# Linear attention and a two-layer MLP on one core: a decode without its magnitude pass, a later range check, and a rewoven first stage

## The chip, the core and the metric

The kernel runs on one NeuronCore of one Trainium2 chip. The metric is device microseconds of one execution. In the profile PE is TensorE's matmul row and PEld its weight loads; DVE is VectorE, ACT ScalarE, POOL GpSimd, and SP the engine that issues most DMAs. Each engine executes its own list of instructions in order.

## The reference

```python
batch, n_heads, seq, head_dim = (4, 8, 768, 48)          # q, k, v, f_logit in float32
f = 1.0 / (1.0 + np.exp(-f_logit))
for t in range(S):
    state = f[:, :, t, :, None] * state + einsum('bhd,bhe->bhde', k[:, :, t], v[:, :, t])
    y[:, :, t] = einsum('bhd,bhde->bhe', q[:, :, t], state)
x = y.transpose(0, 2, 1, 3).reshape(3072, 384)
h = x @ w_in                                              # w_in 384 x 2048
return (maximum(h, 0) ** 2 @ w_out).astype(float32)       # w_out 2048 x 384
```

`w_in` and `w_out` arrive as float64, so the kernel receives them as 64-bit words and has to turn them into float32 itself.

## The kernel before

**Tiling.** The sequence of 768 positions is cut into 6 blocks of 128 (times 4 batches: 512 columns). A unit is one block and one pair of heads (hp): unit n is block n // 4, pair n % 4; units 0 to 3 are block 0, units 4 to 7 block 1. A unit's attention is worked in two chunks of 64 positions: scores inside a chunk, a carried state between chunks. The MLP keeps all weights in SBUF, split into a high and a low part (fp32r), and forms each product of two split numbers from three matmuls. The hidden layer has 16 slices f of 128; a slice's first layer ("up") is 9 matmuls of 128x512, its second layer ("down") 9 more. For block 0, slices 0 and 1 take 3 further matmuls with a fourth weight piece (w4), since block 0's fourth pair of heads is not yet spread over the other x tiles then.

**Decoding a weight** (`decode`, `bits`, `halves`). One 128x384 weight piece comes as 64-bit words, 384 KB. Pieces are numbered (f, i), i = 0 for the first layer and 1 for the second. An early piece costs: on ScalarE a pass |upper word| * 2^-112 with a running sum for a later range check (L138), and a pass that builds the top bits from one byte (L140); on VectorE two shift-and-or passes (L143, L149); on ScalarE a copy to the high part (L166); on VectorE a subtraction for the low part (L168). Late pieces, decoded inside the flow, take L138 and three VectorE passes.

**An order written out by hand.** TensorE, VectorE, ScalarE and SP execute in the order of the program text. Until the MLP is under way, that order is two strings of tokens, FIRST and SECOND; `step` turns each token into instructions. The number is the unit, the slice or the piece:

- `busy`n: n transposes of the identity into an unused bank of TensorE
- `f k L v`: loads of gate logits, keys and queries, all three, values; `j i o`: loads of w4, first-layer and second-layer pieces
- `G` gates (ScalarE); `K` a scan and a product for the keys (VectorE), with a maximum on POOL (L454); `Q` reciprocal, scan and product for the queries (VectorE; the reciprocal needs POOL's maximum)
- `T` transposes of the keys, `N` their copies (ScalarE), `D` state additions, `S` scores, `Y` outputs (TensorE); `M` mask, `C` states (VectorE)
- `r s` crossings: copies of queries and states to the other half of the partitions (ScalarE for block 0, SP DMAs for block 1); `m` moves the fourth pair's share (DMA)
- `H` high part of x (ScalarE), `z` subtracts it by a matmul with a negative identity, `X` low part (ScalarE after a `z`, else VectorE); `h g` spread the fourth pair over the x tiles (DMA)
- `e n t a w`: decode w4; `A I V c J` and `B O Z d P`: the five steps of decoding a first-layer and a second-layer piece, in the order above (J and P are the subtractions)
- `u U` up, `R` square (three ScalarE passes), `E` rest (VectorE subtraction of the high part, L258), `W` down, for block 0's slices 0 to 5

**The flow** (`flow`). After SECOND the three sums of block 0 are copied aside (`keep`, L322), and 90 steps follow: block 1's 16 slices, block 0's other 10, then blocks 2 to 5. Step n does up, square and rest of its slice, and down of the slice two steps back. Two PSUM banks hold the up sums, so up of step n + 2 needs the rest of step n. Everything else hangs on hooks at (step, place): place 0 ahead of up, 0.5 after the squares, 0.7 after rest, 1 after down. Late pieces are decoded there, and the attention of blocks 2 to 5 sits in slots (SLOTS: steps 12, 15, 18, ..., 35, 39, 43, 47, 51, 55, ...), with its loads six steps ahead, gates and keys three ahead, queries and transposes one ahead. In the slot the old unit's outputs and the new one's scores share TensorE; then come the old unit's H and X (and `h g`, the DMAs x<-ys, when the old unit is a block's fourth pair: steps 23, 39, 55), the new one's r, M, C and m.

At the end of the last pass one flag tells whether the inputs were in range; if not, a general path runs (it doesn't here).

Of the kernel before, what the change touches and what calls it, by code (L numbers as in the profile page):

```python
# [22 lines left out]
P = 128  # L23
# [18 lines left out]

LAG = 2
# [19 lines left out]
j0 e0 n0 f0 busy11 busy3 G0 busy2 k0 t0 K0 T0 f1 k1 Q0 G1 v0 K1 S0 N0 D0 M0 i0 A0 I0 T1 L2 o2 L4 C0  # L63
Q1 r0 s0 G2 K2 v1 Y0 N1 H0 z0 X0 D1 S1 B2 i3 Q2 T2 busy3 m1 C1 a0 S2 A3 w0 v2 o1 N2 r1 D2 G4 I3 i1
M1 s1 K4 v3 A1 Y1 D3 H1 C2 s2 z1 X1 r2 m0 f5 m2 S3 r3 o0 B0 V0 M2 k5 L6 v5 busy3 Y2 H2 Q4 r4 v4 C3 s3
G5 I1 T4 z2 X2 M3 busy9 Y3 c0 N4 K5 G6 Q5 V1 H3 busy5 z3 X3 T5 S4 D4 o3 i5 o5 i2 B3 J0 m4 r5 B1 C4 c1 s4 u0
O0 U0 M4 Y4
"""
SECOND = """
J1 Z0 u1 V3 R0 K6 H4 X4 N5 D5 S5 E0 T6 d0 P0 A2 C5 c3 U1 O1 I2 W0 R1 N6 J3 M5 h3 Z1 d1 s5  # L70
Y5 Q6 H5 X5 V2 c2 E1 g3 U3 P1 A5 v6 o4 S6 D6 M6 i4 J2 r6 C6 m5 I5 R3 E3 A4 W1 V5 O3 I4 c5 J5 U2 R2
m6 O2 V4 Z2 s6 v7 r7 Y6 H6 c4 X6 E2 J4 U5 d2 D7 S7 P2 U4 M7 C7 Z3 B4 B5 R4 s7 W2 O4 O5 d3 Z4 Z5 d4
d5 P3 Y7 E4 H7 X7 g7 h7 P4 R5 E5 W3 W4 P5 W5
# [3 lines left out]
class Moe:  # L77


    def __init__(self, ctx, tc, const, sums, out):  # L80
        self.tc, self.nc, self.sums, self.out = tc, tc.nc, sums, out

        self.const, self.raw, self.w, self.ps, self.turns = const, {}, {}, {}, 0
        self.xs, self.spares, self.w4, self.homes, self.held = [], 0, None, {}, None

        self.floor = const.tile([P, 1], F32, name="floor")
        tc.nc.vector.memset(self.floor, -31.0 / 64.0)
# [26 lines left out]
    def decode(self, f, i, scr, early):  # L114

        if early:
# [3 lines left out]
        total = self.sums[:, 2 * f + i : 2 * f + i + 1]  # L120
        yield from self.bits(self.raw[f, i], a, total, early)
        yield from self.parts(f, i, a)

    def bits(self, st, a, total, early):
# [12 lines left out]
        kw = {} if total is None else {"accum_out": total}  # L137
        nc.scalar.activation(a, upper_f, AF.Abs, scale=2.0**-112, **kw)  # L138
        if early:
            nc.scalar.activation(lower, first, AF.Identity, scale=2.0**-5, bias=self.floor[: st.shape[0]])  # L140
        yield
        if early:
            nc.vector.scalar_tensor_tensor(  # L143
                out=h, in0=h, scalar=3, in1=lower, op0=ALU.logical_shift_left, op1=ALU.bitwise_or
            )
        else:
            nc.vector.tensor_scalar(out=h, in0=h, scalar1=3, scalar2=None, op0=ALU.logical_shift_left)
# [4 lines left out]
        if not early:  # L152
            nc.vector.scalar_tensor_tensor(  # L153
                out=h, in0=lower, scalar=29, in1=h, op0=ALU.logical_shift_right, op1=ALU.bitwise_or
            )
# [8 lines left out]
    def halves(self, w, a):  # L164
        nc = self.nc
        nc.scalar.copy(out=w[:, 0], in_=a)  # L166
# [94 lines left out]

    def down(self, f, es=range(NJ)):
# [17 lines left out]
    def flow(self, passes, hooks, opened, closed, held=False):  # L280
# [7 lines left out]
        if held:  # L288
            passes[-1].ends = passes[-1].fs[-2:]
            downs.update({size - 2: [], size - 1: [size - 4, size - 3], size + 1: []})  # L290
        for n in range(size + LAG):
            if n < size:
                self.cur, f = row[n]
                if f == self.cur.fs[0]:
                    opened(self.cur)
                for hook in hooks.get((n, 0), ()):
                    hook()
                self.up(f)
                self.square(f, self.held if held and n == size - 1 else None)
                for hook in hooks.get((n, 0.5), ()):  # L300
                    hook()
                self.rest(f)
                for hook in hooks.get((n, 0.7), ()):
                    hook()
            for m in downs.get(n, ()):
                self.cur, f = row[m]
                if f == self.cur.fs[0]:
                    self.sums_of()
                self.down(f)
                if f == self.cur.fs[-1]:  # L310
                    closed(self.cur)
            for hook in hooks.get((n, 1), ()):
                hook()

    def keep(self):

        part = [
            self.gp.tile([P, NT], F32, tag=f"part{e}", name=f"part{self.cur.blk}_{e}", bufs=1)
            for e in range(NJ)
        ]  # L320
        for e in range(NJ):
            (self.nc.vector.tensor_copy if e % 2 else self.nc.scalar.copy)(out=part[e], in_=self.cur.po[e])  # L322
        return part
# [40 lines left out]
def fast_path(ctx, psum, tc, moe, ident, low, flag, fkqT, vN, w, w4, out):  # L364
# [32 lines left out]
    G.memset(last_kn, 0.0)  # L397

# [7 lines left out]
    class Unit:  # L406
# [74 lines left out]
        def across(self, out, in_, by_dma):  # L481


            (nc.sync.dma_start if by_dma else nc.scalar.copy)(out=out, in_=in_)

        def crossed(self):
            self.rx = self.wk([ROWS, B * C], "rx", 2)
            for c in range(self.blk == 0, NC):
# [4 lines left out]
                    self.blk == 1,  # L493
                )

        def crossed_states(self):
            for c in range(self.blk == 0, NC):
                r = (1 - c) * C
                self.across(self.sx[c * C : c * C + D], self.sp[r : r + D, c], self.blk == 1 and self.hp > 0)
# [132 lines left out]

        def less(self):


            for c in range(NC):
                nc.tensor.matmul(
                    self.py[:, c], lhsT=minus, rhs=self.y[0][:, c], start=False, stop=True,
# [3 lines left out]
        def lower(self):  # L642
            hi, lo = self.y
            if self.blk == 0:
# [13 lines left out]
        def stage(self, letters):  # L658
# [99 lines left out]
    def step(t):  # L758
# [8 lines left out]
        nm = t.rstrip("0123456789")  # L767
        n = int(t[len(nm) :])
        if nm == "busy":
            if 0 not in moe.cur.ph:  # L770
# [338 lines left out]
```

## Time and profile before

| | us |
|---|---|
| median of 3 runs (lowest to highest) | 490.5 (490.15 to 491.19) |
| the profiled execution, its own time | 489.16 |
| its span, first to last instruction | 487.5 |
| PE busy, of the span | 472.8 |
| DVE / ACT / POOL busy | 256.5 / 281.7 / 32.1 |

PE's busy time is modelled: matmuls are pipelined, a 128x512 matmul lasts about 0.39 us in the rows, while its successor begins earlier. In the profile's 40 slices of the span PE stands at 9 tenths or more from the fourth slice on; DVE falls from 9 to 1 tenth over the span.

### The profile page before, as it was taken

The page shows a single profiled execution, that of the slowest core. Times are in us where ns is not written, and L with a number is a line of the kernel's source. Part 1 is how long each engine was busy: PE and PEld are TensorE (multiplying, and loading weights), DVE is VectorE, ACT ScalarE, POOL GpSimd, SP SyncE. Part 2 cuts the span into 40 slices and gives each one's busy share as a digit, 9 for nine tenths or more (in the row PEclk, how much of TensorE's full clock was granted, in tenths as well). Part 3 has the DMA queues.
Part 4 walks back from the last instruction along what each step waited for, and adds up shares of the span by engine and source line. Part 5 has one row for each costly group of instructions (what it writes and reads, how often), then busy time and mean ns, then how long its engine had stood idle before and what let it go on. Part 6 is the DMA issues. An engine that isn't in the chain of part 4 may idle for free. (4 is left out here: it accounts for less than half of the span.)

```text
span 487.5 us, 11465 instructions
## 1 busy us (share of the span) xinstructions
PE 472.8 (97%) x4795; PEld 388.2 (80%) x4795; DVE 256.5 (53%) x474; ACT 281.7 (58%) x570; POOL 32.1 (7%) x82
## 2 busy tenths in 40 slices
PE   5889999999999999999999999999999999999996
PEld 5677787888788888888888888888888888888884
DVE  7999966989985355643437443346343212221111
ACT  4777757887676555644546645555655444544451
POOL 6222010001100000000000000000000000000000
PEclk9999999999999999999999999999999999999998
DMA  8985235566134004232005222004210002100002
GB/s 284 309 284 143 58 103 197 205 200 224 29 95 143 17 6 119 94 101 74 1 2 125 94 93 82 1 1 117 87 26 2 2 0 34 66 0 3 0 0 71
DMA packets 22636, 42.60 MB, mean 87 GB/s; under 512 B 4512, under 2 KB 8128, under 8 KB 22576
## 3 DMA queue, kind: packets, MB, share of 16 engines
q1 hardware_dynamic: 22128, 40.86, 27.1%
q0 software_dynamic: 448, 0.92, 0.8%
q8 instruction: 39, 0.64, 0.5%
q14 instruction: 21, 0.17, 0.1%
HBM read 31.69 MB, written 4.72 MB: 75 GB/s over the span
## 5 line engine op out<-in xcount | busy, mean ns | idle before, releaser
L241 PE MATMUL ph<-x,w 128*128 128x512 f32 x864 | 216.4, 395 | 1.8 <-DVE gl L258 1.4
L241 PEld LDWEIGHTS ph<-x,w 128*128 128x128 f32 x864 | 159.4, 188 | 36.5 <-DVE w L168 1.1
L268 PE MATMUL po<-gh,w 128*128 128x512 f32 x570 | 175.6, 389 | 0.0
L258 DVE TENSOR_TENSOR gl<-ph,gh 128x512 fp32r<-128x512 f32 x95 | 65.6, 691 | 172.1 <-ACT gh L253 171.8
L251 ACT ACTIVATE ph<-ph 128x512 f32<-128x512 f32 x96 | 55.9, 582 | 119.7 <-PE ph L241 119.5
L268 PEld LDWEIGHTS po<-gh,w 128*128 128x128 f32 x570 | 107.0, 188 | 22.2
L268 PE MATMUL po<-gl,w 128*128 128x512 f32 x285 | 111.1, 390 | 0.0
L268 PEld LDWEIGHTS po<-gl,w 128*128 128x128 f32 x285 | 53.5, 188 | 11.2
L252 ACT ACTIVATE ph<-ph 128x512 f32<-128x512 f32 x96 | 55.9, 582 | 3.0
L253 ACT CAST gh<-ph 128x512 fp32r<-128x512 f32 x95 | 55.8, 587 | 3.0
L449 DVE TENSOR_TENSOR_SCAN fkq<-fz,dr 128x520 f32<-128x520 f32 x18 | 22.3, 1236 | 6.3 <-ACT fz L444 6.3
L166 ACT CAST w<-wa 128x384 fp32r<-128x384 f32 (+1 forms) x33 | 16.6, 511 | 15.3 <-DVE wa L153 12.3
L454 POOL TENSOR_SCALAR fkq<-fkq 128x8 f32<-128x8 f32 x18 | 13.2, 735 | 145.1 <-DVE fkq L449 136.6
L463 DVE TENSOR_TENSOR_SCAN fkq<-fz,dz 128x520 f32<-128x520 f32 x18 | 22.3, 1242 | 0.6
L602 PE MATMUL ab_False<-sc,vn 64*48 64x64 f32 (+1 forms) x480 | 20.7, 220 | 0.0
L138 ACT ACTIVATE wa<-raw 128x384 f32<-128x384 f32 (+1 forms) x33 | 18.1, 548 | 4.3 <-DMA raw<-in_w_dram 4.2
L631 ACT CAST x<-ab_False 112x512 fp32r<-112x512 f32 x12 | 7.0, 587 | 22.0 <-PE shared L537 16.0
L611 PE MATMUL ab_False<-rx,sx 48*48 48x64 f32 (+1 forms) x240 | 19.4, 216 | 0.0
L647 DVE TENSOR_TENSOR x<-ab_False,x 112x512 fp32r<-112x512 f32 x12 | 8.3, 692 | 20.2 <-ACT x L631 20.2
L149 DVE SCALAR_TENSOR_TENSOR wa<-raw,wa 128x384 int32<-128x384 int32 (+1 forms) x33 | 17.9, 551 | 0.7
L602 PEld LDWEIGHTS ab_False<-sc,vn 64*48 64x48 f32 (+1 forms) x480 | 18.0, 126 | 0.0
L168 DVE TENSOR_TENSOR w<-wa,w 128x384 fp32r<-128x384 f32 (+1 forms) x33 | 17.9, 545 | 0.0
(138 smaller groups left out, 461.5 us busy)
## 6 DMA issues: line engine op xcount, KB each, us to landing
raw<-in_w_dram SPq DMA_DIRECT2D x32, 384.0 KB, 4.3
fkq<-in_fkqT_dram SPq DMA_DIRECT2D x15, 768.0 KB, 5.8
vn<-in_vN_dram SPq DMA_DIRECT2D x24, 192.0 KB, 4.5
out_dram<-ob SPq DMA_DIRECT2D x14, 256.0 KB, 2.4
fkq<-in_fkqT_dram SPq DMA_DIRECT2D x9, 256.0 KB, 4.6
x<-ys SPq DMA_DIRECT2D x30, 64.0 KB, 2.4
last_kq<-fkq SPq DMA_DIRECT2D x28, 64.5 KB, 2.3
out_dram<-part SPq DMA_DIRECT2D x3, 256.0 KB, 2.4
```

The costliest lines, as they stand in the source:

```text
L138: nc.scalar.activation(a, upper_f, AF.Abs, scale=2.0**-112, **kw)
L149: nc.vector.scalar_tensor_tensor(out=h, in0=upper, scalar=-(1 << 31), in1=h, op0=ALU.bitwise_and, op1=ALU.bitwise_or)
L241: self.nc.tensor.matmul(self.cur.ph[f], lhsT=w[:, i], rhs=x[:, j], start=first and n == 0, stop=last and n == 2)
L251: nc.scalar.activation(ph, ph, AF.Relu)
L252: nc.scalar.activation(ph, ph, AF.Square)
L253: nc.scalar.copy(out=gh, in_=ph)
L258: self.nc.vector.tensor_tensor(out=gl, in0=self.cur.ph.pop(f), in1=gh.bitcast(F32), op=ALU.subtract)
L268: self.nc.tensor.matmul(c.po[e], lhsT=l, rhs=r, start=f == c.fs[0] and i == 0, stop=f in c.ends and i == 2, skip_group_check=len(c.ends) > 1,)
L449: V.tensor_tensor_scan(out=rr[:, ::-1], data0=self.fz[:, NZ * CZ : 0 : -1], data1=dr[:, ::-1], initial=0.0, op0=ALU.mult, op1=ALU.add,)
L463: V.tensor_tensor_scan(out=pp, data0=self.fz[:, : NZ * CZ], data1=dz, initial=0.0, op0=ALU.mult, op1=ALU.add)
L602: nc.tensor.matmul(to[:m], lhsT=self.vn[rows, b, h * D : h * D + m], rhs=self.sc[rows, h, b], start=b == 0, stop=none and c == 0 and b == ...
L611: nc.tensor.matmul(to[:m], lhsT=s[rows, b * D : b * D + m], rhs=q[rows], start=False, stop=b == B - 1,)
```

## The change

1. **Early pieces without the magnitude pass.** `bits` for an early piece no longer issues L138; its ScalarE pass writes the top bits straight into the output, and two VectorE passes combine them with the upper word.
2. **A later check.** The 12 early pieces are remembered; in the flow, at steps 32, 34, ..., 54, the words of one piece are loaded again (two DMAs of 256 KB and 128 KB), and at steps 34, 36, ..., 56, place 0.7, VectorE masks the exponents and takes a minimum and a maximum. `verdict` compares these with two bounds.
3. **More matmuls with the negative identity.** Units 4 and 5 get a `z` too, so their `X` goes to ScalarE; slices 0, 1 and 3 of block 0 use `F` (one matmul) and `l` (a ScalarE copy) in place of `E`.
4. **Crossings of block 1** go to ScalarE; a mark ' at a token sends three of the high-part copies (d3', d4', d5') to VectorE, and lets B5' use another scratch buffer.
5. **The order.** FIRST and SECOND are new; `flow` yields between its parts, so that tokens `x` run its first parts inside SECOND, and `p` makes the copies of `keep` one by one. The loads of slices 6 and 7 are tokens now.

```diff
 FIRST (after):
+f0 busy11 G0 j0 k0 v0 f1 busy3 v1 e0 k1 K0 L2 n0 L4 o0 busy4 G1 Q0 busy4 T0 busy4 N0 D0
+K1 S0 C0 Q1 T1 i0 N1 D1 G2 M0 s0 r0 S1 K2 G4 Y0 busy4 v2 t0 H0 r1 busy4 B0 T2
+A0 Q2 N2 z0 D2 M1 v3 C1 busy4 X0 S2 C2 f5 I0 i1 s1 v5 Y1 i3 busy4 m2 G5 O0 busy3
+r2 V0 H1 m0 z1 A1 M2 D3 i2 X1 o1 v4 s2 k5 m1 K4 r3 c0 Y2 C3 S3 a0 i5 L6
+H2 M3
 SECOND (after):
+z2 T4 J0 I1 s3 X2 Y3 A3 H3 A2 N4 w0 z3 V1 X3 o2 u0 Q4 K5 U0 D4 c1 r4 J1
+C4 S4 M4 R0 B1 v6 Z0 u1 s4 Y4 h3 d0 I2 T5 H4 N5 Q5 F0 z4 X4 o3 l0 I3 P0
+r5 V3 o5 U1 G6 i6 D5 C5 S5 s5 i4 M5 R1 c3 W0 Y5 K6 J3 V2 F1 H5 l1 c2 T6
+Q6 N6 J2 v7 O1 m6 o4 g3 z5 U3 X5 m5 i7 D6 S6 C6 A5 U2 r6 M6 R3 o6 Z1 F3
+I5 s6 Y6 d1 P1 A4 H6 W1 m4 V5 I4 B2 X6 c5 V4 D7 l3 J5 R2 C7 S7 r7 U5 s7
+M7 E2 c4 O2 J4 Y7 Z2 B3 H7 U4 d2 O3 X7 B5' P2 h7 W2 B4 Z3 O4 d3' P3 O5 R4
+R5 Z4 d4' E4 P4 E5 Z5 W3 W4 g7 o7 d5' P5 x1 x2 x3 x4 W5 p1 p2 p0 x6 x7 x8
+x9 x10 x12 x13 x14 x15 x16 x17 x18 x19 x20 x21 x22 x23
@@ bits @@
-        nc.scalar.activation(a, upper_f, AF.Abs, scale=2.0**-112, **kw)
         if early:
-            nc.scalar.activation(lower, first, AF.Identity, scale=2.0**-5, bias=...)
+            nc.scalar.activation(h, first, AF.Identity, scale=2.0**-5, bias=...)
+            yield
+            nc.vector.scalar_tensor_tensor(
+                out=h, in0=upper, scalar=3, in1=h, op0=ALU.logical_shift_left, op1=ALU.bitwise_or)
+            yield
+            nc.vector.scalar_tensor_tensor(
+                out=h, in0=upper, scalar=(1 << 30) - 1, in1=h, op0=ALU.bitwise_or, op1=ALU.bitwise_and)
+            yield
+            return
@@ halves @@
-        nc.scalar.copy(out=w[:, 0], in_=a)
+        (nc.vector.tensor_copy if self.second else nc.scalar.copy)(out=w[:, 0], in_=a)
+        self.second = False
@@ new in Moe @@
+    def less(self, f, minus):
+        gh, _ = self.cur.g[f]
+        self.nc.tensor.matmul(self.cur.ph[f], lhsT=minus, rhs=gh, start=False, stop=True, ...)
+    def rest_less(self, f):
+        _, gl = self.cur.g[f]
+        self.nc.scalar.copy(out=gl, in_=self.cur.ph.pop(f))
+    def check_load(self, w):
+        f, i = self.unchecked.pop(0)
+        self.words2 = []
+        for n, cut in enumerate((slice(0, 256), slice(256, DM))):
+            t = self.gp.tile([P, NT], F32, tag=f"part{n}", name=f"check{n}_{f}_{i}", bufs=1)
+            t = t[:, : 2 * (cut.stop - cut.start)]
+            self.nc.sync.dma_start(t.bitcast(I64), w[f, i][:, cut])
+            self.words2.append((t, cut))
+    def check(self):
+        nc, n = self.nc, self.checked
+        self.checked += 1
+        a = self.gp.tile([P, NT], F32, tag="part2", name=f"checked{n}", bufs=1)[:, :DM]
+        words, self.words2 = self.words2, ()
+        for t, cut in words:
+            upper = t.bitcast(I32).rearrange("p (n two) -> p n two", two=2)[:, :, 1]
+            nc.vector.tensor_scalar(out=a.bitcast(I32)[:, cut], in0=upper, scalar1=EXPONENTS, ...)
+        for k, op in enumerate((ALU.min, ALU.max)):
+            at = 2 * LO * k + n
+            nc.vector.tensor_reduce(out=self.ends[:, at : at + 1], in_=a, axis=..., op=op)
@@ fast_path @@
+    G.memset(moe.sums, 0.0)
+    G.memset(moe.ends, 1.0)
+        for k in range(2 * LO):
+            n = CHECKS + 2 * k                       # CHECKS = 32
+            hook(n, 0.5, lambda: moe.unchecked and moe.check_load(w))
+            hook(n + 2, 0.7, lambda: moe.words2 and moe.check())
```

## Rows read from the trace of the kernel before

**Rows 1.** Busy time by stretch; columns PE, PEld, DVE, ACT, POOL, clock, DMA.
```profile
4.40:34.10 29.70, 23.73 (x565) 19.19 (x563) 27.91 (x45) 20.03 (x48) 9.03 (x18) 1.00 0.95 309
34.10:74.10 40.00, 39.11 (x582) 30.87 (x577) 33.65 (x71) 27.85 (x62) 5.40 (x11) 1.00 0.43 122
160.00:480.00 320.00, 320.00 (x2966) 264.62 (x2964) 122.07 (x203) 165.90 (x309) 9.89 (x31) 1.00 0.15 43
```

**Rows 2.** Timeline of PE; columns start, length, line, instruction, count, idle before.
```profile
1.59 3.67 PE L773 MATMUL ph<-ident 128*128 128x128 f32 x16 [1.59 <-POOL ident masks.py:199]
...
9.60 1.13 PE L553 MATMUL ds<-fkq 48*64 48x64 f32 x32 [1.23 <-DVE fkq L466]
...
20.81 0.69 PE L553 MATMUL ds<-fkq 48*64 48x64 f32 x32
...
30.06 0.34 PE L602 MATMUL first_py<-sc,vn 64*48 64x64 f32 x9 [0.39 <-DVE sc L567]
...
31.89 0.49 PE L637 MATMUL first_py<-ys,minus 112*112 112x256 f32 x2
32.23 0.60 PE L511 MATMUL pk<-ident,fkq 128*128 128x128 f32 x4
...
34.14 0.50 PE L241 MATMUL ph<-x,w 128*128 128x512 f32 x1
35.12 2.14 PE L241 MATMUL ph<-x,w 128*128 128x512 f32 x8 [0.47 <-DVE w L168]
...
71.95 4.24 PE L241 MATMUL ph<-x,w 128*128 128x512 f32 x18
76.79 2.37 PE L241 MATMUL ph<-x,w 128*128 128x512 f32 x9 [0.59 <-DVE gl L258]
```

**Rows 3.** Timeline of DVE in the first stage.
```profile
22.14 1.24 DVE L449 TENSOR_TENSOR_SCAN fkq<-fz,dr 128x520 f32<-128x520 f32 x1 [0.32 <-ACT fz L444]
...
24.03 0.35 DVE L582 TENSOR_TENSOR sp<-ds,fkq 112x192 f32<-112x192 f32 x1
...
24.68 0.55 DVE L149 SCALAR_TENSOR_TENSOR wa<-raw,wa 128x384 int32<-128x384 int32 x1
25.16 0.68 DVE L567 TENSOR_TENSOR sc<-ds,mask 128x512 f32<-128x512 f32 x1
25.75 0.20 DVE L461 RECIPROCAL dz<-fkq 128x8 f32<-128x8 f32 x1
...
27.87 0.35 DVE L582 TENSOR_TENSOR sp<-ds,last_kq 112x192 f32<-112x192 f32 x1
...
34.52 0.55 DVE L168 TENSOR_TENSOR w<-wa,w 128x384 fp32r<-128x384 f32 x1
...
68.83 0.55 DVE L168 TENSOR_TENSOR w<-wa,w 128x384 fp32r<-128x384 f32 x1
```

**Rows 4.** Timeline of POOL at the first maximum.
```profile
6.63 0.67 POOL L454 TENSOR_SCALAR fkq<-fkq 128x8 f32<-128x8 f32 x1 [0.33 <-POOL x L697]
```

**Rows 5.** Instructions of line L147 on DVE; ns minimum, median, maximum.
```profile
L147 DVE TENSOR_SCALAR wa<-wa x20: 350/353/360, 76.6 to 134.7; 128x384 int32<-128x384 int32 x20
```

**Rows 6.** Groups by line on ACT, 0 to 74.1 us; busy, mean ns, idle before.
```profile
L138 ACT ACTIVATE wa<-raw 128x384 f32<-128x384 f32 (+1 forms) x13 | 7.1, 550 | 4.3 <-DMA raw<-in_w_dram 4.2
```

**Rows 7.** Timeline of SP's queue near step 39 of the flow.
```profile
256.58 3.75 SPq L654 DMA_DIRECT2D x<-ys  x6
...
261.65 0.60 SPq L437 DMA_DIRECT2D fkq<-in_fkqT_dram  x1
```

**Rows 8.** DMA issues by line: count, KB each, median us to landing.
```profile
out_dram<-ob SPq DMA_DIRECT2D x14, 256.0 KB, 2.4
...
fkq<-in_fkqT_dram SPq DMA_DIRECT2D x9, 256.0 KB, 4.6
```

**Rows 9.** Timeline of DVE at step 40 of the flow.
```profile
260.78 1.24 DVE L449 TENSOR_TENSOR_SCAN fkq<-fz,dr 128x520 f32<-128x520 f32 x1 [0.75 <-ACT fz L444]
```

**Rows 10.** Timeline of PE behind step 42 of the flow.
```profile
267.50 0.60 PE L511 MATMUL shared<-ident,fkq 128*128 128x128 f32 x4
```

More of the change, by code (lines that the diff above doesn't have):

```diff
@@ L151, in bits @@
         )
[L152 to L155, printed above, removed]
+        nc.vector.scalar_tensor_tensor(
+            out=h, in0=lower, scalar=29, in1=h, op0=ALU.logical_shift_right, op1=ALU.bitwise_or
+        )
         yield
@@ L305, in flow @@
             for m in downs.get(n, ()):
-                self.cur, f = row[m]
-                if f == self.cur.fs[0]:
+                c, f = row[m]
+                self.cur = c
+                if f == c.fs[0]:
                     self.sums_of()
                 self.down(f)
[L310 to L323, printed above, removed]
+                if f == c.fs[-1]:
+                    closed(c)
@@ new lines, in flow, with keep @@
+            at(n, 1)
+            yield
+    def keep(self, part, e):
+        ob = self.gp.tile([P, NT], F32, tag=f"part{e}", name=f"part{self.cur.blk}_{e}", bufs=1)
+        (self.nc.vector.tensor_copy if e % 2 else self.nc.scalar.copy)(out=ob, in_=self.cur.po[e])
+        part[e] = ob
+    def check_load(self, w):
[6 more added lines that the diff above has]
+            self.words2.append((t, cut))
@@ L325, in finish @@
+    checked, words2 = 0, ()
     def finish(self, dst, part=None, third=None):
@@ L773, in step @@
                 nc.tensor.transpose(out=moe.cur.ph[0][:, 0:P], in_=ident, identity=ident)
+        elif nm == "x":
+            next(row)
+        elif nm == "p":
+            moe.cur = first
+            moe.keep(part, n)
         elif nm in ("i", "o"):
@@ L784, in step, with product @@
             if nm in "AB":
-                decoding[n, i] = moe.decode(n, i, pro, True)
+                decoding[n, i] = moe.decode(n, i, pro, True, not mark)
+            if nm in "cd":
+                moe.second = bool(mark)
             next(decoding[n, i])
-        elif nm == "u":
+        elif nm in "uURFlEW":
+            moe.cur = first
+            product(nm, n)
+        else:
+            unit(n).stage(nm, mark)
+    def product(nm, n):
+        if nm == "u":
             moe.up(n, last=False)
@@ L814, in fast_path @@
         moe.sums_of()
-        for t in SECOND.split():
-            step(t)
-        part = moe.keep()
         whole = half[0] + half[1]
@@ L894, in fast_path @@
         moe.hold()
-        moe.flow(passes, hooks, opened, closed, held=True)
+        row = moe.flow(passes, hooks, opened, closed, held=True)
+        for t in SECOND.split():
+            step(t)
+        for _ in row:
+            pass
         return passes[-1], read[0]
@@ L1016, in block @@
             c = moe.begin(nm, x, list(range(NF)), sums)
-            moe.flow([c], {}, lambda c: None, closed, held)
+            for _ in moe.flow([c], {}, lambda c: None, closed, held):
+                pass
         with tc.For_i(0, NBLK - 1, 1) as blk:
```

113 lines of the change are left out of this document (68 added, 45 removed).

## The prediction

> **What bounds the kernel now.** I read the busy times by stretch first. From 160 us to 480 us TensorE is busy for 320.00 of 320 us, while VectorE works 122 us and ScalarE 166 us of them [rows 1]. Nothing that shortens another engine's list there can show, and an addition to one shows only if it makes TensorE wait. The stretch from 4.4 to 34.1 us is the opposite: VectorE is busy for 27.91 of 29.70 us, and TensorE's 23.73 us hold padding. From 34.1 to 74.1 us both are close to full, 39.11 and 33.65 of 40 us [rows 1].
>
> The list of TensorE's instructions gives the places [rows 2]. It begins with 16 padding transposes. The first product of block 0's first layer starts at 34.14 us and its run stalls 0.47 us on a weight, so the dense work starts in effect at 34.61 us. Block 1's flow starts at 71.95 us; its third group waits 0.59 us. The time is therefore the moment at which dense work starts, plus TensorE's work, plus stalls. VectorE's list sets that moment.
>
> **Prices on VectorE** come from one unbroken stretch, start to start [rows 3]: K (scan and product) 24.03 - 22.14 = 1.89 us; C in block 0 0.65; one shift-and-or of a weight 0.48; M (mask) 0.59; Q (reciprocal, scan, product) 27.87 - 25.75 = 2.12. The three passes of the 112x256 weight I take at 256/384 of 0.48, 0.32 each.
>
> **Start of the dense work.** Before, VectorE's list up to the step J0 that the stall waits for has 5 K (9.45), 5 Q (10.60), 4 M (2.36), 4 C (2.60), three small passes (0.96), 5 shift-ors (2.40) and J0 (0.48): 28.85 us, done at 34.52 + 0.55 = 35.07 [rows 3]. So 6.2 us are start and gaps. The new order asks less before u0: u0 stands behind z3, which follows Y3, which needs M3. Up to M3 VectorE has 4 K (7.56), 3 Q (6.36), 4 M (2.36), 4 C (2.60), two small passes (0.64) and 3 shift-ors (1.44): 20.96 us. I keep 6.2 us of start and gaps. The load f0 now goes ahead of the weight load j0, but Q0 needs POOL's maximum, which began at 6.63 us right behind POOL's own clearing of x and took 0.67 us [rows 4]. Two more clearings now stand ahead of it, so the early load buys between 0.2 us lost and 0.8 us gained; I take nothing. M3 ends at 27.2. Before, Y3 started at 30.06 and z3 started at 31.89 with 0.34 us until the next transposes at 32.23 [rows 2]: 2.2 us, and about 0.2 us between M3 and Y3. The new u0 starts at 27.2 + 0.2 + 2.2 = 29.6 us, 5.0 us earlier.
>
> **What that moves behind it.** T5, D4 and S4 ran before u0 and now run after: 34.14 - 32.23 = 1.9 us, a wait of about 0.2 in it, so 1.7 us. New on TensorE are three products F (18 products take 4.24 us from 71.95 us on, so (4.24 - 0.39)/17 = 0.226 us each) and z4, z5 (0.34 each): 1.4 us. Together +3.1 us.
>
> **Stalls.** TensorE idles 40.00 - 39.11 = 0.89 us in the second stretch [rows 1], 0.47 of it already counted; the other 0.42 and the 0.59 us at 76.79 us can go, since x2 now puts block 1's first group ahead of W5, and x3 its squares ahead of the copies p. That is -1.0 us. New stalls come from the two lists running side by side. TensorE's list from 29.6 us: 71.95 - 34.61 - 0.42 = 36.9 before, plus 3.1, plus 2.0 for block 1's first group, ends at 71.6 us. VectorE's after M3: 69.4 (68.83 + 0.55, the early stage's last weight part) - 35.07 [rows 3] = 34.3 us before; plus Q4, K5, Q5, two shift-ors, one small pass and J0 (7.9); minus five passes of about 0.6 us that go to ScalarE (E0, E1, E3, X4, X5; 3.0); plus three copies d3', d4', d5' at 0.35 to 0.55 us, taken as 0.4, near the one-source pass of the same 128x384 [rows 5]: 1.2. That makes 40.4 with its old waits inside, so P5 at 67.6 us, when W5 needs it by 69.6. Two lists with 2 us to spare in 40 will hold each other up: between 0 and 3 us; I take 0.5, since the old pair lost 0.4. The early stage in sum: -5.0 + 3.1 - 1.0 + 0.5 = -2.4 us.
>
> **Edits that I cost at nothing.** The magnitude pass is 13 x 0.55 = 7.1 us of ScalarE [rows 6], which has 20.0 of 29.7 and 27.9 of 40 us filled before 74.1 us [rows 1]; it hides behind VectorE and TensorE. The room is used: 14 crossings of block 1 go from SP's queue to ScalarE, each smaller than that pass, so under 7.7 us, and five of VectorE's passes join them. If ScalarE were late instead, one of its waits, at most 0.55 us each, would show at the bank of a product. Fourteen fewer DMAs on SP free its queue; the weight loads i6 to o7, which only the flow decodes, move up into that room.
>
> **The later check.** Eleven checks run at steps 34 to 54 of the flow, some 230 to 320 us into the span (an estimate, from 72 us at step 0 and 258 at step 40): twelve loads are made, but the load at step n stands ahead of the check of the same step and replaces the words list, so each check reads the words loaded in its own step. One check is one AND over 384 columns in two pieces and two reductions. The trace has no such reduction; between the one-source pass (0.35 us [rows 5]) and a shift-or (0.48) for each of the three it is 1.1 to 1.5 us, 12 to 16 us in all. VectorE has 198 free us in 160 to 480 us; without that cover all of it would show.
>
> The order of SP's queue is another matter. At step 39 SP issues six x<-ys at 256.58 us behind VectorE's ys, then two moves, and its next load went out at 261.65 us [rows 7]. The check's two loads of step 40 stand exactly there: 261.65 and 262.25. A 256 KB transfer lands 2.4 us (writes) to 4.6 us (fkq) after its issue [rows 8]: 264.7 to 266.9 for the second. VectorE, which executes in order, stands at that check from about 260 us on. Queued behind it are K of the next unit, at 260.78 us before [rows 9], and the rest pass of step 41. After landing there remain 0.9 to 1.3 us of check and 1.89 of K, so K ends at 267.5 to 270.1; TensorE's transposes of that K ran at 267.50 and the product whose bank the rest pass frees right behind them [rows 10]. The price is 0.2 (0.7 for the rest pass, 0.5 of it covered) to 2.9 us; I take 1.2, a landing near 3.3 us. No other of the checked steps has six x<-ys ahead of its loads; step 44 has outputs and moves. I take nothing there, with up to 2 us as the other end.
>
> **Sum.** -2.4 + 1.2 = -1.2 us. The profiled execution took 489.16 us with a span of 487.5; the median shown is 490.5, 1.3 us above, and the difference is carried over: 489.3 us.
>
> **Rivals.**
> A, the forecast: 489.3 us, itself 488.0 to 490.4. Chance 0.38.
>
> B, no wait at step 40, because the small loads land in 2.4 us, and the lists interlock as ordered: the early stage gives 2.5 to 4 us, 487.2 us. For it: SP's queue is empty for long stretches after 262 us. Against: two full lists. Chance 0.24.
>
> C, the early gain is eaten by TensorE's clock. The granted clock reads 1.00 from the start [rows 1], yet 32 score products took 1.13 us at 9.60 us and 0.69 at 20.81 [rows 2], so the rows themselves show the lower of the two levels (1.2 and 2.4 GHz) until about 20 us. If it stays low as long, Y0 (2.2, twice about 1.1), eight transposes (8 x 0.229 = 1.8, from 16 in 3.67 us), T2 (0.9), z0 (0.7) and D2 (1.1) run from 15.3 to 22.0 us (sums of estimates from these rows). VectorE reaches C2 behind 3 K, 3 Q, 2 M, 2 C and two small passes, 15.2 us by the prices above, plus about 5.2 of start and gaps: at 20.4. It waits some 1.6 us. All later steps follow, and 0.8 us of gain is left against 1.2 of the check: 490.9 us. For it: the 16 first transposes did not lift the clock. Against: the new order pads from 1.59 us with 22 and then without a gap to the first scores. Chance 0.23.
> On this the Trainium skill ("TensorE: Matmul & The Clock Gate", Part 4: PE-mode transpose) says that a transpose does not count as TensorE being busy in the way a product does, which speaks against padding with transposes. By that rule the added padding buys nothing and C it is, at 490.9 us; the trace agrees as far as the 16 go.
>
> D, slower: the check's loads at steps 40 and 44 both land late (4.6 us), because they stand in one queue behind x<-ys, moves and outputs, and cost 2.9 and 2 us: -2.4 + 4.9 = +2.5, 493.0 us. It decides from about 3.5 us of added waits on. For it: SP's order is fixed. Against: at step 44 no x<-ys stands ahead, so the loads go out sooner. Chance 0.15.
>
> That the magnitude pass, taken alone, does nothing for the time is part of A and C.
>
> **The numbers.** What a measurement of this kernel can tell from no change is about 0.2%, 1.0 us. A is beyond it on the fast side in 6 of 10 and within it otherwise, B fast, C within in 7 of 10 and else slower, D slower: faster 0.23 + 0.24 + 0.01 = 0.48, within 0.30, slower 0.22. The range from B's far end (-4.5 us, 486.0) to 492.0 leaves out half of D and little else.
>
> **What would show it.** u0 at 29 to 30 us in TensorE's list (later than 32 us: the start is wrong); score products near 0.69 us already at 10 us (else C); block 1's first group done by 71 to 72.5 us, TensorE's idle time below 1.5 us in 34 to 74 us (more: lists interlocked); at step 40, near 258 us, one wait of VectorE on the check's load and a wait of TensorE of about 1 us; no idle TensorE elsewhere in 160 to 480 us. A time below 486 would mean that the early stage held waits hidden in TensorE's modelled busy time; one above 492, that checks stall in several places.

## The result and the profile after

| | us |
|---|---|
| after, median of 4 runs (lowest to highest) | 496.18 (494.47 to 498.30) |
| before, in the same session | 490.32 |
| ratio, 95% interval | 1.0122 (1.0078 to 1.0166) |
| the profiled execution of after, its span | 498.30, 496.6 |

The change costs 5.9 us where 1.2 us were to be gained. The profiled execution is the slowest of the four, 2.1 us above their median, and that of before was 1.3 us below its own, so the two traces differ by more than the medians do.

Busy time by stretch of after (same columns as [rows 1]):

```profile
4.40:34.10 29.70, 19.96 (x492) 17.09 (x494) 24.43 (x41) 14.29 (x32) 7.43 (x15) 0.86 0.94 312
34.10:74.10 40.00, 35.55 (x634) 27.90 (x631) 30.02 (x60) 30.34 (x66) 6.59 (x14) 0.94 0.38 101
160.00:480.00 320.00, 318.86 (x3078) 263.35 (x3077) 138.57 (x255) 166.89 (x313) 9.97 (x32) 1.00 0.22 60
```

Three things are new. VectorE, busy for 27.91 us of the first stretch before, is now busy for 24.43: it waits. TensorE idles 4.45 us in the second (0.89 before). And TensorE is no longer full from 160 to 480 us: 1.14 us are missing there.

TensorE's timeline of after, against [rows 2]:

```profile
9.35 0.66 PE L619 MATMUL ds<-fkq 48*64 48x64 f32 x30
...
13.88 1.13 PE L619 MATMUL ds<-fkq 48*64 48x64 f32 x32 [0.16 <-DVE fkq L534]
...
26.69 0.27 PE L845 MATMUL ph<-ident 128*128 128x128 f32 x1 [2.82 <-issue]
...
28.87 0.27 PE L619 MATMUL ds<-last_kq 48*64 48x64 f32 x1
...
33.08 0.35 PE L668 MATMUL first_py<-sc,vn 64*48 64x64 f32 x2 [1.60 <-issue]
...
36.27 3.57 PE L261 MATMUL ph<-x,w 128*128 128x512 f32 x9
39.67 0.86 PE L261 MATMUL ph<-ys,w 112*128 112x512 f32 x3
40.46 0.68 PE L603 MATMUL ds<-vn,kn 64*64 64x48 f32 x32
42.40 0.69 PE L619 MATMUL ds<-fkq 48*64 48x64 f32 x32 [1.26 <-DVE state L655]
...
50.28 0.69 PE L619 MATMUL ds<-fkq 48*64 48x64 f32 x32 [1.26 <-DVE state L655]
...
66.40 0.79 PE L619 MATMUL ds<-last_kq 48*64 48x64 f32 x32 [1.26 <-DVE state L655]
...
78.79 2.20 PE L261 MATMUL ph<-x,w 128*128 128x512 f32 x9
```

The first product starts at 36.27 us, 6.7 us later than forecast, and its nine take 39.67 - 36.27 = 3.40 us where nine take 2.04 at block 1's first group (78.79 to 80.83). Before it TensorE stood twice with nothing recorded that it waited for ("issue"). Then come three waits of 1.26 us, all of score products S, for `state`, the result of step C on VectorE. In the code after, C4, C5 and C7 stand between their unit's D and S; before, S came first. D, S and C share one PSUM tile, `ds`: by the code D writes its columns 0 to 191, C reads these, and S writes the columns behind them. S takes no value from C, but it waits until VectorE is through with the tile, and TensorE's whole list behind S waits with it.

VectorE's timeline of after, against [rows 3]:

```profile
22.30 0.36 DVE L648 TENSOR_TENSOR sp<-ds,fkq 112x192 f32<-112x192 f32 x1 [2.29 <-PE ds L619]
...
27.93 0.36 DVE L648 TENSOR_TENSOR sp<-ds,last_kq 112x192 f32<-112x192 f32 x1 [1.01 <-PE ds L603]
28.33 0.35 DVE L655 TENSOR_TENSOR state<-sp,ds 112x192 f32<-112x192 f32 x1
29.76 0.69 DVE L633 TENSOR_TENSOR sc<-ds,mask 128x512 f32<-128x512 f32 x1 [1.07 <-PE ds L619]
...
41.21 0.35 DVE L655 TENSOR_TENSOR state<-sp,ds 112x192 f32<-112x192 f32 x1 [2.67 <-PE ds L603]
...
41.99 0.35 DVE L655 TENSOR_TENSOR state<-sp,ds 112x192 f32<-112x192 f32 x1
```

The first of these are C2, C3 (two rows) and M3; the last two are the first and the last pass of C4 behind D4. M3 ends at 29.76 + 0.69 = 30.45 us; the forecast had 27.2. VectorE's waits for TensorE up to there are 4.37 us. At C4 each engine waits for the other: VectorE 2.67 us for D4, then TensorE 1.26 us for C4.

The check at step 40, SP's queue and then VectorE and TensorE of after, against [rows 7, 9, 10]:

```profile
264.59 4.47 SPq L723 DMA_DIRECT2D x<-ys  x6
269.17 1.15 SPq L542 DMA_DIRECT2D last_kq<-fkq  x2
270.37 1.05 SPq L371 DMA_DIRECT2D check<-in_w_dram  x2
```

```profile
273.26 0.56 DVE L382 TENSOR_SCALAR checked<-check 128x256 int32<-128x256 int32 x2 [5.23 <-DMA check<-in_w_dram]
273.86 1.01 DVE L387 TENSOR_REDUCE ends<-checked 128x1 f32<-128x384 f32 x2
274.79 1.23 DVE L517 TENSOR_TENSOR_SCAN fkq<-fz,dr 128x520 f32<-128x520 f32 x1
```

```profile
276.80 0.66 PE L577 MATMUL shared<-ident,fkq 128*128 128x128 f32 x4 [1.14 <-DVE fkq L523]
```

This is what was forecast, instruction by instruction: the load behind six x<-ys, VectorE standing at the check, K behind it, TensorE's transposes late by 1.14 us. VectorE stood ready 5.23 us before its start at 273.26, so from 268.03 us on, while the loads went out at 270.37 us. No other check made TensorE wait.

To see where time is lost and won back, I count MLP products (both layers) along TensorE's list and compare the start of the k-th with that of before (us, negative is earlier; e5 and e12 are experiments below):

```
k          before    after       e5      e12
1           34.14    +2.12    +0.26    -3.41
10          37.09    +2.58    -0.62    -4.29
61          56.84   +10.29    +3.44    -0.08
146         79.91    +7.95    +1.09    -2.42
701        224.21    +7.99    +1.11    -2.35
901        276.91    +9.59    +1.13    -2.33
1734       482.51    +9.59    +1.13    -2.32
```

After loses 2.6 us until the tenth product, 7.7 between the 10th and the 61st, wins 2.3 back until the 146th, and loses 1.6 at step 40. Elsewhere nothing moves. The zero of this table is before's trace, which is 1.3 us faster than before's median.

### The profile page after: what moved, and what is told of

Its sections match the earlier page's. It is cut to its first block, busy times and chain, and to the rows that moved or that the text cites. A ratio compares the mean times of both kernels' runs of the same rounds, so it can differ in the third digit from the quotient of the medians.

```text
span 496.6 us, 11530 instructions
## 1 busy us (share of the span) xinstructions
PE 474.5 (96%) x4811; PEld 390.5 (79%) x4811; DVE 269.1 (54%) x519; ACT 281.7 (57%) x562; POOL 31.7 (6%) x84
## 5 line engine op out<-in xcount | busy, mean ns | idle before, releaser
L261 PEld LDWEIGHTS ph<-x,w 128*128 128x128 f32 x864 | 160.5, 189 | 35.1 <-ACT w L185 1.0
L278 DVE TENSOR_TENSOR gl<-ph,gh 128x512 fp32r<-128x512 f32 x92 | 63.6, 691 | 152.0 <-ACT gh L273 151.4
L185 ACT CAST w<-wa 128x384 fp32r<-128x384 f32 (+1 forms) x30 | 15.3, 512 | 13.0 <-DVE wa L172 12.1
L551 ACT COPY sx<-sp 48x208 f32<-48x208 f32 x44 | 16.0, 364 | 1.0
L677 PEld LDWEIGHTS ab_False<-rx,sx 48*48 48x48 f32 (+1 forms) x240 | 16.6, 127 | 0.0
```

What stands on the lines that cost most here:

```text
L261: self.nc.tensor.matmul(self.cur.ph[f], lhsT=w[:, i], rhs=x[:, j], start=first and n == 0, stop=last and n == 2)
L278: self.nc.vector.tensor_tensor(out=gl, in0=self.cur.ph.pop(f), in1=gh.bitcast(F32), op=ALU.subtract)
L551: {"": nc.scalar.copy, "'": V.tensor_copy, "^": nc.sync.dma_start}[self.mark](out=out, in_=in_)
L677: nc.tensor.matmul(to[:m], lhsT=s[rows, b * D : b * D + m], rhs=q[rows], start=False, stop=b == B - 1,)
```

## Experiments

Theory 1 was: the loss is the three S that wait for C, and a fourth pair, C3 ahead of S3, on the path to the first product; the check at step 40 is the forecast's. Rivals: the new decode or its check itself; TensorE's stands, by late instructions behind the weight loads; TensorE's clock. All comparisons are with the kernel before in the same session (490.36 to 490.67 us).

**r1: old order, new decode and check.**

```diff
-FIRST, SECOND of after
+FIRST, SECOND of before (block 1's crossings by DMA, marked r4^ s5^ ...; keep and i6 o6 i7 o7 last)
```

> The changed kernel's code (decode without the magnitude pass, later check) under the order of the kernel before, crossings of block 1 by DMA as before, the four loads of slices 6 and 7 and the three copies p at the end of SECOND. Theory A, the loss lies in the new order: 490.3 us of before plus the check's own wait of about 1.1 us at step 40, so 490.5 to 492. Rival B, the decode or the check costs the time: near 496 us.

Measured: 492.99 us, ratio 1.0059 (1.0036 to 1.0082). TensorE's waits between 225 and 330 us:

```profile
PE shared L575 <- DVE fkq L521: 2.3, 1, 2.3
```

Some 2.6 us slower, about as much as the wait at step 40. By the products' starts the trace loses 2.7 us there and 1.5 in the first stage, against a trace of before that is 1.3 us under its median. Freeing ScalarE of the magnitude pass shows no gain by itself in the old order.

**r2: S ahead of C again.**

```diff
-Y2 C3 S3 ...  C4 S4 ...  D5 C5 S5 ...  C7 S7
+Y2 S3 C3 ...  S4 C4 ...  D5 S5 C5 ...  S7 C7
```

> The changed kernel with the scores S3, S4, S5 and S7 ahead of the states C3, C4, C5 and C7 in the order, as the kernel before had them. Theory A: S writes the PSUM tile that C reads, so S behind C waits for VectorE; the three waits of 1.26 us at S4, S5 and S7 go, and the time falls by about 3.8 us, to 491 to 494 us. Rival B: VectorE sets the pace of that stretch anyway and TensorE waits elsewhere instead: 495.5 to 496.5 us.

Measured: 489.31 us, ratio 0.9966 (0.9944 to 0.9988), 6.9 us less than after. TensorE's waits from 36 to 490 us:

```profile
PE shared L577 <- DVE fkq L523: 1.4, 1, 1.4
PE ph L261 <- DVE gl L278: 0.8, 1, 0.8
```

No S waits. Exchanging four pairs of neighbouring tokens turns the slowdown into a small gain. It is 3.1 us more than the three waits held, and the time lies below the range that was expected.

**r3: no later check** (the range check of the early pieces is left out).

```diff
-            hook(n, 0.5, lambda: moe.unchecked and moe.check_load(w))
-            hook(n + 2, 0.7, lambda: moe.words2 and moe.check())
```

> The changed kernel without the later check's loads and passes (the range check of the early pieces is left out). Theory A: only the wait of 1.1 us at step 40 goes, 495.1 us (494.5 to 495.7), and VectorE falls by about 12 us of busy time. Rival B: the twelve further loads cost more than that single wait: under 494 us.

Measured: 492.61 us, ratio 1.0044 (1.0017 to 1.0070). TensorE is busy for 105.00 of 105 us between 225 and 330 us (103.86 in after). Its three S waits, from the view of TensorE's waits from 30 us on, are still there:

```profile
PE ds L619 <- DVE state L655: 3.8, 3, 1.3
```

The check was a part of the loss, not its main cause. But the time is 3.6 us below after's, more than the 1.60 us of step 40 and within the rival's range. That rival's reason isn't borne out: after's loads go out from 219 us on, and r3's trace is ahead of after's long before, at the tenth product already (2.4 us earlier than before, where after is 2.6 later), with no stand above 0.7 us. The edit touches no instruction of that stage; why its trace has no long stand isn't shown.

**r4: late weight loads.** i3, i2, o1, i5 and L6 are held back (a mark * at a load makes it wait for VectorE's list).

```diff
-Y1 i3 ... D3 i2 X1 o1 v4 ... a0 i5 L6 H2 M3
+Y1 ... V0 i3* ... D3 X1 v4 ... a0 H2 M3 i2* o1* i5* L6
```

> The changed kernel with five loads of the first stage (i3, i2, o1, i5, L6) held back, the pieces by a one-word clearing on VectorE ahead of each: i3 behind V0, the others behind M3. Theory A: TensorE's waits of 2.8 and 1.6 us that the profile puts to issue, near 24 and 32 us, are waits for its own code, whose block arrives late because the DMA engines are full; with less in flight both fall below 0.5 us, the clock doesn't fall to half at 32 to 39 us, and the time is 490 to 493 us. Rival B: these waits don't hang on the data in flight; both stay within 0.7 us of their size, and the time is 495.5 to 498 us.

Measured: 495.61 us, ratio 1.0089 (1.0058 to 1.0120). TensorE's longest waits from 20 us on:

```profile
PE ds L619 <- DVE state L655: 4.7, 4, 1.3
PE ph L261 <- ACT ys L714: 1.8, 1, 1.8
PE shared L577 <- DVE fkq L523: 1.4, 1, 1.4
```

The stands shrank to 0.3 us and the first product came at 31.70 us, but now all four S wait, X3 makes a new wait, the check remains, and the granted clock falls to half all the same, from 35.9 to 46.2 us. So the stands alone don't explain the time. What they are worth is left to e11 and e12.

**e5: check loads sooner**, on top of r2.

```diff
-            hook(n, 0.5, lambda: moe.unchecked and moe.check_load(w))
+            hook(n, 1, lambda: moe.unchecked and moe.check_load(w))
```

At place 0.5 a step's load stands ahead of its own check at 0.7 and is the one which that check reads. At place 1 it stands behind, so the next check, two steps later, reads it.

> Scores ahead of states as in the run with S3, S4, S5 and S7 moved (489.31 us), and besides each later check's words are loaded at place 1 of a step instead of place 0.5, so they leave SP's queue two steps ahead of the check that reads them and step 40's pair stands ahead of the six x<-ys. Theory (TensorE's wait at step 40 is the check behind its own load): that wait goes, 1.1 to 1.4 us, and the time is 487.9 us, ratio about 0.995. Rival (the load only uncovers the next thing VectorE is late with, or two words lists alive at once hold up the decode of the late pieces): a wait of TensorE stays somewhere in 225 to 330 us and the time is 489.0 to 489.6 us.

Measured: 487.32 us, ratio 0.9932 (0.9911 to 0.9953), 2.0 us less than r2 by the medians; the two intervals overlap. TensorE from 225 to 330 us:

```profile
225.00:330.00 105.00, 105.00 (x1091) 86.76 (x1093) 59.76 (x118) 57.30 (x108) 4.33 (x13) 1.00 0.32 93
```

The wait is gone and the table shows 0.02 us between the 701st and the 901st product. That is the firmer evidence: the check costs TensorE nothing once its words are there.

**e6: old decode in the new order**, with r2's S ahead of C: the magnitude pass on ScalarE is back, the later loads and checks are out. Two of the changed lines:

```diff
+            nc.scalar.activation(a, upper_f, AF.Abs, scale=2.0**-112, **kw)
-            self.unchecked.append((f, i))
```

> The order with S ahead of C (489.31 us), with early pieces decoded as before the change: the magnitude pass on ScalarE with its running sum is back, and the later loads and checks are gone. Theory (the magnitude pass hides on ScalarE in the new order too, as it did in the old one, and the later check costs 1.3 us at step 40): 487.9 us, the same as with the check's loads sent sooner, and no wait of TensorE at step 40. Rival 1 (taking the magnitude pass away is what lets ScalarE take 14 crossings and five other passes): ScalarE is late in 20 to 75 us, block 1's first group ends 2 us or more later than with S ahead of C alone (77.3 us), and the time is 489.5 to 492 us.

Measured: 488.52 us, ratio 0.9962 (0.9943 to 0.9982). It overlaps with e5's interval: leaving the magnitude pass out is worth 1.2 us by the medians, and by the intervals perhaps nothing.

**e7: the kernel before with C ahead of S.**

```diff
-T5 S4 D4 ... B1 C4 ...  D5 S5 ... A2 C5 ...  D7 S7 P2 U4 M7 C7
+T5 D4 C4 S4 ... B1 ...  D5 C5 S5 ... A2 ...  D7 C7 S7 P2 U4 M7
```

> The kernel before, with the state passes C4, C5 and C7 put between the state additions D and the scores S of their unit, as the change has them. Theory (S writes the PSUM tile that C reads, so TensorE stands until VectorE has done C; it cost about 5 us in the changed order for four of them): three waits of TensorE of 1.0 to 1.3 us with S, and a time of 490.3 + 3 to 4 = 493.5 to 494.5 us. Rival (the stage is paced by VectorE's list, which TensorE's wait doesn't lengthen; the loss was in the rest of the new order): the waits show but the time stays within 491.3 us.

Measured: 495.77 us, ratio 1.0107 (1.0088 to 1.0126). TensorE's waits from 36 to 80 us:

```profile
PE ds L555 <- DVE state L591: 5.6, 3, 2.4
```

C ahead of S for three units, made in the kernel before, alone reproduces a slowdown of this size: 5.1 us by the medians, 5.6 us in three waits, more than was expected. Two of them (2.41 and 1.89 us) exceed 1.26 us; at the longer one VectorE began its first pass of C4 only at 34.57 us, 0.8 us after D4 had ended. The granted clock was at half from 35.1 to 41.9 us too, which before's trace hasn't. With r2 this shows the order of S and C as a cause in both directions; the fourth pair of theory 1, C3 ahead of S3, is another matter (see below).

**e8: no added products with the negative identity**, on top of e5.

```diff
-F0 z4 X4 o3 l0 ...  F1 H5 l1 ...  z5 U3 X5 ...  F3 ... l3
+X4 o3 E0 ...        H5 E1 ...     U3 X5 ...     ... E3
```

> The kernel with S ahead of C and the check's loads sent sooner, but without the added products with the negative identity: X4 and X5 and the rests of slices 0, 1 and 3 go back to VectorE (no F0, F1, F3, z4, z5). Theory (TensorE sets the pace of 36 to 75 us once S no longer waits, so its 5 products are a cost of 1.4 us): 1.0 to 1.5 us less than with them, 486.5 us if that is 487.9. Rival (VectorE sets the pace there, and five passes of 0.6 us, 3.0 us, come back on it): 1 to 3 us more than with them, 489 to 491 us.

Measured: 491.75 us, ratio 1.0041 (1.0015 to 1.0067), 4.4 us more than e5. The rival was right, and beyond its range: five passes back on VectorE cost more than their products on TensorE. TensorE's longest wait in 20 to 80 us was 2.5 us of a D (L603).

**e9: more padding**, on top of e5: 14 more transposes where TensorE idled between 23 and 33 us.

```diff
-O0 busy3 ...  Y2 S3 ...        J0 I1 s3 X2 Y3 ...        w0 z3
+O0 busy7 ...  Y2 busy3 S3 ...  J0 I1 busy3 s3 X2 Y3 ...  w0 busy4 z3
```

> The fastest version so far (scores ahead of states, check's loads sent sooner; 487.32 us), with 14 more padding transposes where TensorE idles between 23 and 33 us: 4 after Y1, 3 ahead of S3, 3 ahead of Y3, 4 ahead of z3. Theory (in some executions the clock falls to half between 26 and 40 us because TensorE stands there, and that costs 2 to 3 us; padding holds it up): no half clock after 21 us in the profile and a median of 485.5 to 486.5 us with a narrower spread. Rival 1 (transposes do not hold the clock, or its fall is set by what came before): half clock still appears after 21 us and the time stays 487 to 488 us. Rival 2 (the padding itself stands in the way, 14 at 0.11 to 0.23 us, 1.5 to 3 us at most): 488 to 490 us.

Measured: 487.98 us, ratio 0.9932 (0.9903 to 0.9960). In the profiled execution the granted clock stayed at 1.00 from 18.9 us on, and the spread narrowed (486.87 to 489.07, against 486.31 to 489.84), but the median didn't fall. Whether the padding took what the clock gave, or the clock gave nothing, this run doesn't tell.

**e10: less padding**, on top of e5: the seven runs of padding behind the first 14 transposes are out (27 transposes).

```diff
-o0 busy4 G1 Q0 busy4 T0 busy4 N0 ...  Y0 busy4 v2 ...  C1 busy4 X0 ...  i3 busy4 m2 G5 O0 busy3
+o0 G1 Q0 T0 N0 ...                    Y0 v2 ...        C1 X0 ...        i3 m2 G5 O0
```

> The same fastest version without the padding in the middle: the seven runs of 3 or 4 transposes after the first 14 are taken out (27 transposes). Theory (transposes lift the clock: it rose at 5 us after nothing but padding): the clock rises later or falls oftener, the first product comes 2 us or more later than 34.4 us, and the time is 489.5 to 492 us. Rival (they count for nothing and only fill TensorE's list): 487.3 us or up to 1 us less, with the same clock.

Measured: 490.45 us, ratio 0.9990 (0.9965 to 1.0014), 3.1 us more than e5. TensorE's first transposes and a run of scores, first of e10, then of after:

```profile
1.59 3.25 PE L845 MATMUL ph<-ident 128*128 128x128 f32 x14 [1.59 <-POOL ident masks.py:199]
6.81 1.12 PE L577 MATMUL pk<-ident,fkq 128*128 128x128 f32 x4 [1.97 <-DVE fkq L523]
9.76 1.14 PE L619 MATMUL ds<-fkq 48*64 48x64 f32 x30
```

```profile
1.59 4.28 PE L845 MATMUL ph<-ident 128*128 128x128 f32 x22 [1.59 <-POOL ident masks.py:199]
6.78 0.66 PE L577 MATMUL pk<-ident,fkq 128*128 128x128 f32 x4 [0.91 <-DVE fkq L523]
```

With 22 transposes ahead of them the same four take 0.66 us, with 14 they take 1.12. In all ten traces with 22 the granted clock rose between 5.0 and 7.6 us, after nothing but transposes; in e10 it rose at 22.8. With the old order's 16 it rose at 4.3 us in r1 and e7, where the four took 0.66 and 0.73 us, and in before it shows no rise until 20.8. So padding made of nothing but transposes can bring the higher level (2.4 GHz of the two), and the middle padding is worth 3 us here. The first product came only 0.5 us later than in e5 (34.9 against 34.4), not the 2 us expected; behind it e10's clock is at half until 39.8 us, e5's until 29.7.

**e11: late loads**, on top of e5 (r4's edit).

```diff
-Y1 i3 ... D3 i2 X1 o1 v4 ... a0 i5 L6 H2 M3
+Y1 ... V0 i3* ... D3 X1 v4 ... a0 H2 M3 i2* o1* i5* L6
```

> The same fastest version with the weight loads i3, i2, o1, i5 and L6 held back behind VectorE's list, as in the earlier run with late loads, so that the DMA engines are less full between 22 and 28 us, where TensorE stood 2.5 us with nothing waited for (23.94 to 26.41 us). Theory (that stand is TensorE's own instructions arriving late behind the weight loads, and it delays the first product by 2.5 us in the executions that have it): no stand above 0.7 us, first product at 31.5 to 32 us, median 485.5 to 486.5 us. Rival (the stand is a symptom that comes and goes, or later weights arrive too late for their decode): 487 to 489 us.

Measured: 490.07 us, ratio 0.9990 (0.9966 to 1.0014). TensorE, and then ScalarE, of e11:

```profile
30.33 2.24 PE L261 MATMUL ph<-x,w 128*128 128x512 f32 x9
35.36 0.96 PE L261 MATMUL ph<-ys,w 112*128 112x512 f32 x3 [2.79 <-ACT ys L714]
```

```profile
33.60 0.63 ACT L154 ACTIVATE wa<-raw,floor 128x384 int32<-128x384 uint8 x1 [3.65 <-DVE fkq L523]
...
34.70 0.60 ACT L714 CAST ys<-first_py 112x512 fp32r<-112x512 f32 x1
```

No stand above 0.6 us, and the first product at 30.33 us, near the forecast's 29.6. But ScalarE reads the held load i2 in A2, stands there 3.65 us (the row names VectorE's product, long done), and X3 behind it makes TensorE wait 2.79 us. One move made its own new wait.

**e12: A2 behind r4**, on top of e11.

```diff
-A3 H3 A2 N4 w0 z3 V1 X3 o2 u0 Q4 K5 U0 D4 c1 r4 J1
+A3 H3 N4 w0 z3 V1 X3 o2 u0 Q4 K5 U0 D4 c1 r4 A2 J1
```

> As the fastest version with weight loads held back (490.07 us, first product at 30.33 us and no stand of TensorE before it), with one token moved: A2, ScalarE's pass over the held load i2, on which ScalarE stood 3.65 us ahead of the low part X3 that TensorE's third product group waited 2.79 us for, now stands behind r4. Theory (stand and clock apart, the forecast's start near 30 us is real, and only the held load took it back): that wait goes and the time is 490.07 - 2.8 = 487.3 us at most, 486 to 487 us if the first product stays near 30.3 us. Rival (VectorE's list sets block 1's start whatever the dense work does at 30 us): the early gain is waited away between 36 and 74 us and the time is 488 to 490 us.

Measured: 486.64 us (486.15 to 487.47), ratio 0.9922 (0.9904 to 0.9940): 3.8 us faster than before, 9.5 faster than after, and the steadiest of the new orders. TensorE of e12:

```profile
30.40 0.49 PE L706 MATMUL first_py<-ys,minus 112*112 112x256 f32 x2 [0.68 <-ACT ys L697]
30.73 2.24 PE L261 MATMUL ph<-x,w 128*128 128x512 f32 x9
32.81 0.86 PE L261 MATMUL ph<-ys,w 112*128 112x512 f32 x3
...
68.42 2.20 PE L261 MATMUL ph<-x,w 128*128 128x512 f32 x9
```

M3 of e12 on VectorE:

```profile
27.50 0.68 DVE L633 TENSOR_TENSOR sc<-ds,mask 128x512 f32<-128x512 f32 x1
```

## Why the prediction was wrong

It forecast 489.3 us (486.0 to 492.0); after takes 496.2.

**The step that failed is the one on stalls**: "Two lists with 2 us to spare in 40 will hold each other up: between 0 and 3 us; I take 0.5". It compared the lengths of two lists and never followed one tile through the order. C ahead of S on one PSUM tile is a round trip TensorE, VectorE, TensorE with nothing between, whatever spare time the lists have. Three of them cost 3.8 us by the rows, more than that step's own upper end; between the 10th and the 61st product, after needs 27.46 us where e5, with S first, needs 23.80. The diff showed it: the tokens stand side by side. The size could be had from prices at hand: the forecast had C of block 0, two passes, at 0.65 us; C of block 1 has four, of which three follow D, from 41.21 to 41.99 + 0.35 = 42.34 us in after, 1.13 of the 1.26 us.

**The start of dense work** was to come at 29.6 us and came at 36.27. The sum of VectorE's prices was sound: in e12, M3 ends at 27.50 + 0.68 = 28.2 us (1.0 later than forecast) and the first product starts at 30.73 (1.1 later). What the step left out was TensorE as a cause. M3's delay in after is 3.25 us: TensorE's stand of 2.82 us held D3, so that C3 waited 1.01 us, and held Y2 and S3 behind D3, so that M3 waited 1.07. C3 ahead of S3 held nothing in this execution: S3 began at 28.87 us with no idle time before it, when C3 was through (28.33 + 0.35 = 28.68). In r3 and r4, without that stand, S3 does wait for `state`, 0.54 and 0.88 us. From M3's end to the first product, 5.8 us passed instead of 2.4: the second stand (1.60 us), and the clock, granted at half from 32.3 to 39.2 us, for Y3 and z3. It also stretched the nine products by 1.36 us; while they ran, the busy table of after reads (PEclk 0.50):

```profile
36.00:38.00 2.00, 2.00 (x7) 1.61 (x7) 0.47 (x2) 1.98 (x6) 0.49 (x2) 0.50 0.42 70
```

**Moved work** was sized at +3.1 and old stalls at -1.0. With S first, e5 needs 1.7 us more than before from the 10th to the 146th product, and e12 1.9, against +2.6 with the 0.5 of new stalls: right within a microsecond. The early stage in sum is -2.42 us in e12, where the forecast said -2.4, but that agreement is partly luck: the start gained 4.29 us there (at the tenth product) against 5.0 forecast, which the smaller moved work made up for, and the zero is a trace of before that is 1.3 us fast. By the medians e12, which has no wait for the check, is 3.8 us faster. So the terms fit, each within a microsecond, an order with S first, the five loads held back and A2 moved; they don't fit the one that was measured.

**The check** was right in place and size: forecast +1.2 us (0.2 to 2.9), 1.14 us in the wait row and 1.60 in the products' starts; VectorE started 2.9 us after the first of the two loads went out, and one check takes 274.79 - 273.26 = 1.5 us, the forecast's upper end. Rival D expected a second wait at step 44; there is none. Rival B lacked the first. The count was off by one: the trace has eleven loads and ten checks, not twelve and eleven. The mark at B5' does more than choose a buffer; by the code it sends that piece down the late path, with the magnitude pass (L165, at 71.58 us), so it isn't among the pieces remembered. And the piece loaded first, at step 32, is replaced before any check reads it, so in after its range is never checked; in e5 all eleven are.

**The magnitude pass** at nothing was right in r1 and nearly so in e6. The passes that moved to ScalarE are worth more than was thought: e8 lost 4.4 us without them.

**Rival C** was half right. The scores at 9.35 us took 0.66 us, so the clock had risen early, against C. Then it fell: 13.88 us shows 1.13. C2 waited 2.29 us, where C had put 1.6. In e12 the same wait is 2.17 us, and that kernel is fast; so it doesn't set after apart. On the Trainium skill's statement ("TensorE: Matmul & The Clock Gate", Part 4: PE-mode transpose) that a transpose doesn't count as a busy TensorE in the way a product does, the measurement decides otherwise for this kernel: the four transposes at 6.78 us took 0.66 us after nothing but transposes, 1.12 in e10 with fewer of them. Before's own 16, on which rival C leaned, were one draw: the same 16 were followed by the higher clock in r1 and e7.

**The stands** follow the instruction queue. The DMA view of after from 23.5 to 26.7 us, while TensorE stood, and of e12 from 20 to 23 us:

```profile
q1 hardware_dynamic: 531, 1.10, 99.1%
q8 instruction: 1, 0.02, 2.3%
```

```profile
q1 hardware_dynamic: 255, 0.42, 48.1%
q8 instruction: 1, 0.02, 2.0%
```

In after, e5 and e10 (stands of 2.82, 2.47 and 1.71 us) no instruction packet moved between 20 and 23 us and one did between 23.5 and 25.5; the other new orders (r2, r3, r4, e6, e8, e9, e11, e12) had theirs between 20 and 23 us, and no stand above 1.0. The weight loads were held back in three of these only, so holding them back goes with an early block but isn't needed for it. Packet by packet the tie is closer (us; the packets are those of queue q8 in the traces):

```
        packet from   to       stand ends   its length
after   24.09         25.27    26.69        2.82
after   30.57         31.69    33.08        1.60
e5      23.74         25.03    26.41        2.47
e10     24.11         25.23    26.62        1.71
e9      28.41         29.49    30.73        0.97
r3      22.18         23.14    24.60        0.67
```

In the 14 traces TensorE has 19 waits above 0.3 us that are put to "issue", and each of them ends 1.2 to 1.6 us after the end of such a packet. That fits a wait for instructions; nothing else that is recorded here does. The Trainium skill's page "Runtime: NRT & Kernel Launch", section "Instruction fetch mechanics", says that an engine fetches the next block of instructions while it executes the current one, mostly hidden; if these stands are that fetch, it wasn't hidden here. **Open** is what makes the packet late: no run moved it by itself. And r2 gained 3.1 us beyond the 3.8 of three waits; since C3 ahead of S3 held nothing in after's trace, the stands and the clock of the first stage are left for it, and how much each took isn't settled.

## What to carry to other kernels

Where two engines run orders written by hand, go through each exchanged pair of steps and ask which tile both touch: a reader of another engine placed between two writers of one PSUM tile is a round trip in the bound engine's list, however much spare time a comparison of busy times shows. A load that a later step waits for should leave ahead of the transfers that it would queue behind: sent at the end of the step two before its check instead of in the check's own step, it left before the six x<-ys, and TensorE's wait was gone (2 us by the medians). When an order leaves a stage with several close limits, expect the first repair to show the next wait, and repair that before judging the idea (e11, e12).

## What the runs showed of the hardware that was not expected

- The granted clock rose after padding of transposes alone (22 of them from 1.59 us on; 16 in two traces of three; not 14 in the one with 14), fell again while small products and waits alternated, and rose a second time; in six kernels a further low stretch of 3.4 to 10.2 us came between 26 and 46 us, and in e10 one of 13.7. Where it rose between 4 and 8 us, it had fallen again by 14.5 us in every trace.
- Executions of one program differ: of the new orders by 1.3 us (e12, six executions) to 7 us (e8, twelve), and of the kernel before by 7.2 us too (488.98 to 496.18 in 29 executions beside e9 to e11). One trace of such a kernel is one draw.
- TensorE's waits for nothing that the profile names ended 1.2 to 1.6 us after a packet of the instruction queue, all 19 of them.
